# Matrix products over halves of the array's rows: inverse transforms, kernel rows and state sums of a long-convolution layer and its gradients, regrouped

## The chip, the cores and the metric

The kernel runs on one core of a Trainium2 chip. Its matrix engine (PE) multiplies, the vector engine (DVE) and the scalar engine (ACT) do elementwise work and empty the matrix engine's accumulators (PSUM), the general-purpose engine (POOL) and the sync engine (SP) mostly issue transfers. The metric is the device time of one execution in microseconds. The kernel before takes 607.57 us, the median of three runs (607.13 to 607.59).

## The reference, cut to what matters

The layer takes `u` of 2048 positions by 512 channels, normalises each position, and multiplies two branches: a state-space convolution, and a dense pair `w1` (512 by 1792) and `w2` with SiLU. The program returns the output and the gradients of eleven inputs.

```python
xn = layernorm(u)                                 # 2048 x 512
dt = exp(log_dt)[:, None]                         # 512 x 1
P  = exp((dt * A)[:, :, None] * arange(2048))     # 512 channels x 128 states x 2048 steps, complex
K  = einsum("dn,dnl,dn->dl", C, P, dt * B).real   # the convolution kernel, 512 x 2048
y  = irfft(rfft(pad(xn.T)) * rfft(pad(K)))[:, :2048].T + xn * Dskip
g  = silu(silu(xn @ w1) @ w2)
out = u + y * g
grads = vjp(out, grad_out)                        # of u, A, B, C, log_dt, Dskip, w1, w2
```

## The kernel before, in words

**Program order.** Every part of the work is a Python generator, called a stream, with a letter. A stream gives control back after each small piece: a group of matrix products, or the copy that empties a PSUM tile. `PLAN` holds seven strings, one for each section of the program, and `play` resumes the streams in the order of the letters. This is the order of each engine's instructions; nothing reorders them later. `SLOTS` says which buffer each new tile takes. `WAYS` says, stream by stream, which of the PSUM copies go to ACT (`A`) and which to DVE (`D`); all of them stand at one line of the profile for each engine (L112 for ACT, L113 for DVE).

**Forward section (to about 215 us).** The dense branch (`gen_ffn_fwd`: L751 and L768), the tables of powers, the kernel rows and the forward convolution run interleaved. The channels go in four bands of 128. A transform of length 4096 (`dft_fwd`) is a product over 128 positions (L405), sixteen transposes (L415), and a product with a small table `F2` (L425), which is 128 rows by 64 columns and is used twice, once for each half of the output's partitions. After it a spectrum tile has, on its 128 partitions, two halves of 64; each half holds 16 frequencies of 4 channels, so a 128-row slice of a spectrum holds 8 channels, 4 in each half.

**Inverse transforms** (`dft_inv`, 4 forward and 8 backward). The first step (L440) takes a spectrum slice of 128 by 128 as the stationary operand and a table `I2` of 128 by 256 as the moving one. `I2` carries the transform of 16 frequencies for 8 channels; a mask makes it zero wherever row and column belong to different channels, so it is zero between the two halves too. Four slices fill a PSUM tile of 1024 elements for each partition; one copy empties it into `dB`. The second step is L453.

**Kernel rows** (`gen_powers`, `gen_kernel_rows`). The 2048 powers of a channel come from 21 exponents `E` and 32 exponents `Y`. `Y[h]` (tile `YD`) is laid out as 16 groups of 4 channels: state on the partitions, then group, exponent, channel. For each group, L639 multiplies `Y` (128 states by 32 exponents of 4 channels) with `W` (21 exponents of 4 channels), four times, and accumulates. Of the 128 by 84 results those where the two channels are the same are wanted. Four groups fill a PSUM tile `ps_k` of 336 elements, and a copy moves it to `Xr`. The tables `SEL`, one for each of the 4 channels of a group, then pick and shift the wanted rows by further products (L651). The pool `pt` has one buffer, which `ps_k`, `ps_e` and later `psS` share in turn.

**Backward convolution (about 215 to 400 us).** Streams `D`, `B` and `E` transform the gradient, multiply spectra on DVE (`cplx_mul`, L466 to L474) and transform back, twice for each band. Between them run the backward products of the dense branch (L1149, L1169).

**State gradients (about 400 to 560 us).** `gen_ssm_fold` gathers the kernel's gradient (`GE`), sums it by products with `FO` (L953), and an ACT copy spreads it over 4 channels (`Gf`, L956). `gen_ssm_v` masks it with `MK` (`Gb`, L988, DVE), multiplies it with the transposed `Y` table (`YT`, L998, 168 columns for each of 256 products) and copies the result to `Vb`. DVE multiplies by `E` (`Tp`, L1013), and `gen_ssm_sums` adds the 21 exponents up by products with the identity into `psS` (L1031 to L1035: 43 products for each of 16 groups); ACT copies to `Sa` (L1037), and `gen_ssm_grads` works out the gradients. The two weight-gradient products (L1202, L1231) run beside this and on to the end, where the layer norm's gradient is finished (L1269 to L1293).

Of the kernel before, what the change touches and what calls it, by code (L numbers as in the profile page):

```python
# [31 lines left out]
XFXPPRRXRRFXXXJXQRRXFRRCCXXPRRPPJJPRCRCXRPFQRCCCQXXPCJCCQFFFQQFFFRFCCPPFFCCQFRQFFQQXFQCXQFFCFFFRRRCFFCCRRCJCCRRCCCRCRCPC
RCRXXFFQRCRXXXQQCRCXRCCXCXRQQRRRRXRQRXQQXQQFXRXPFXXXFFFCJCPFRFPPCCCCFFRRPPFXRQRRRFFFXUFQQQFFXCCFCCFQFCRRCUCQCCCFRQQRCCQR
QFCQFCCRRCCRRRRRCCRCCRRCRCCCCRRFFFFCRCCCCCRRRCRRCCRC/FCCCCFFCCCCCFGGFGGCCCCCGGGGGGFGFGCCCCGGGGGFFCFFFFFCFCCFFGWGGCCCCHHF
FGGGCCCCCFGCCFFCCCCCWCCCCHWGGWWWCCCHHHHHWWCWWWCCWCCWDMWWWDGDDWWDWWDDDWLWWWWDWDDDLCLLLMMMMDDDWWDD/dDDaDaddDDdDsAAAEADDDDD
BAaBAAaABBDEaAAsADDDAsABBBAABBBoooAoAAABBBsAAAEDBBADBlDBDAlAlBBBBBxBDABBBBOAooAxxDDoBDBABoAAOBBEBOBOOOOOlldlxaBxxBooBBBo
sxOooBBBBDDDDxoxoxBdDaxBBDBAABBBdBBBDDAAaBBBBOBBBBBBAABBsAAAOADDDEDAAADBAADOOoBsOdOBABOBAoAoAAABBBDoxAOAOODBABosBBABDxDB
BAoOBDDDDAADDAAODxDDooodDAOOOdoBBaOBBOBoBBoOOdodDDxDEDxxBxaBBBsAAAOOaAABBABABBDBDAABDBDBoBoBBxxDOOExDDDsxAABBxBABBaBABBs
AAABBABBEOOOxOxBAABBBABBABAxBBBxxaaaBBBBBAsBBBBBBBBBBBBAAAxxBBBAAABBBBBAAAABBBABdBd/xxdAdNssxxsYaAsAAAAYYNAAAAAAAxxNNAAA
AAAAAAYAAAAAANNxVVVVAAxVVVVVVAATTVVxxVVxVVYxVVTYYxxxxNNNTTTTNSVVVVVVVYxSx/VTTSTSVTTVVVVVhhVVVSSVVVVVVVTTTYYttTtSthVTTNTT  # L40
tttYwwtSVVVVSgVVVVtStthVtNNwNNwNVTwTTVVVwwNNNNZZTgStZSZZVtVVwVZtZtYYYhgvvYvvVZTTTTVVwVwZZVZVVSVVVVVYtTSTTTVvvwVttVVSVVVV
TTTvSTwgVVVhVVSYvtZZttwYYTTVThTVZtVVvZvZtVVVVVTSvvhVVVVSVVtSwwVVvVwTTTTwtTYYYVVVVZSSVTVVVZTTYtZZttZtvtVVVSVtTSVVVVvvVTgT
TZYZYTTwTVVVZZwvVVVZVZZVZhwwwSwStghtVVggVVSStwZgvVVZZVVhTTTvZZZTvTvTTSvvTvtSSStttvgthZvvwwttZZttZgZwwwZhZZZZvZvZZtttwwt/
wttivtiikkhvkwwikktkmkkmkkkmttmmmkimmvgkvvviigvvvvvwwkkmvttvkkkkwwvvkmkwkgmwwwkkimmkkmkmvmkmmmvvvvvvvvvmvkkkkmmmvmvvvvvv
vvvv
# [16 lines left out]

WAYS = """J=DAAAADDD;
F=AADAAAAAAAAADAAADAAAAAAAAAAADDAAAAAAADADAAAADAAADAAAAAAAADDAADADDDDDDDAA;
X=AAAADAAAAAAAAADAAAAAAAAAADAAAAAAAAAAAAAD;
R=AAAAAAADAADDADAAAAAAAAAAAAAAAADDDDDDDDAADAAADAAAAADDAAAAADAAAAAADAAAAAAADAAAADDA;
C=AADDAAAAAAAAAAAAAAAADDAAAAAAADAAADAAADAAAAADDADAADADDDADAAAAAAAA;
W=DDDDADDDDDDDDD;  # L70
D=AAAADDAAAADAAAAAAAAAAAAAADAAAADAADAAAAAA;
d=DDADAAAA;
# [1372 lines left out]
```

## Time and profile before

| | before |
|---|---|
| median of 3 runs | 607.57 us |
| the profiled execution | 606.76 us |
| its span, first to last instruction | 605.0 us |
| granted TensorE clock, mean over the span | 0.989 |
| instructions | 14383 |

The profiled execution lies 0.8 us below the median, and its span 1.8 us below its own time. In the profile a group of instructions is named by line, engine, operation and tiles; behind it stand how many there were, the time that they kept the engine busy and the mean time of one. A matrix product's printed duration has a modelled end and includes the way through the array: consecutive products overlap, and what one costs in a dense stretch is read from when the next one starts. In the timeline the first column is the start of a run of equal instructions, the second its length from the first start to the last modelled end; so the start of one row less the start of the row before it is what the earlier run cost. `PEld` is the loading of stationary operands.

### The profile page before, as it was taken

How to read it: one execution, taken by the hardware profiler on the slowest of the kernel's cores; microseconds unless marked ns; L12 is line 12 of the kernel's file. 1: busy time of each engine (PE TensorE's matmuls, PEld its weight loads, DVE VectorE, ACT ScalarE, POOL GpSimd, SP SyncE). 2: the span in 40 equal slices, each digit the busy share in tenths (PEclk: the TensorE clock that was granted, in tenths of full speed). 3: DMA queues.
4: the chain of work that ended last, by engine and by line, in shares of the span. 5: the costliest groups of instructions: out<-in, count | busy, mean ns of one | idle time of the engine just before them, and what ended most of it. 6: DMA issues, size and time to landing. Idle time of an engine off the chain costs nothing. (4 is left out here: it accounts for less than half of the span.)

```text
span 605.0 us, 14383 instructions
## 1 busy us (share of the span) xinstructions
PE 560.1 (93%) x5861; PEld 425.3 (70%) x5884; DVE 533.0 (88%) x906; ACT 443.2 (73%) x552; POOL 77.5 (13%) x171
## 2 busy tenths in 40 slices
PE   1597989999999989999999999999799999999995
PEld 1354758677777686786787767775787888795864
DVE  8989999999999889999998799568759889978894
ACT  7989989999998669998787864641575456434661
POOL 6211001010101120000000100000000202123121
PEclk9988999999999999999999999999999999999998
DMA  9896678676658598959877798797999999999993
GB/s 267 260 306 203 254 245 287 225 249 236 248 160 331 216 297 322 330 126 294 276 232 250 233 296 253 210 230 181 242 202 207 232 252 150 246 207 270 309 242 132
DMA packets 156066, 146.83 MB, mean 243 GB/s; under 512 B 79520, under 2 KB 133024, under 8 KB 152416
## 3 DMA queue, kind: packets, MB, share of 16 engines
q1 hardware_dynamic: 146688, 123.10, 72.1%
q0 software_dynamic: 6768, 19.93, 9.2%
q10 hardware_dynamic: 2544, 2.88, 1.5%
q8 instruction: 46, 0.75, 0.5%
q14 instruction: 20, 0.16, 0.1%
HBM read 63.44 MB, written 62.00 MB: 207 GB/s over the span
## 5 line engine op out<-in xcount | busy, mean ns | idle before, releaser
L112 ACT CAST dA<-ps_s 128x1024 bf16<-128x1024 f32 x86 | 86.3, 1037 | 7.6 <-PE ps_s L425 4.0
L751 PE MATMUL ps_h<-XT,W 128*128 128x256 bf16 x448 | 57.4, 279 | 6.2 <-ACT hT L112 4.6
L112 ACT CAST Vb<-ps_v 128x672 bf16<-128x672 f32 x49 | 34.1, 723 | 37.3 <-PE ps_v L998 32.7
L1149 PE MATMUL ps_da<-doT,W 128*128 128x256 bf16 x448 | 55.2, 273 | 1.2 <-ACT pd_s L112 1.1
L1013 DVE TENSOR_TENSOR Tp<-Vb,Eb 128x1344 bf16<-128x1344 bf16 x64 | 51.0, 850 | 5.9 <-ACT Vb L112 5.9
L768 PE MATMUL ps_o<-W,aT 128*128 128x512 bf16 x214 | 52.7, 399 | 1.1 <-issue 0.9
L112 ACT CAST dB<-ps_i 128x1024 bf16<-128x1024 f32 x41 | 41.1, 1031 | 16.4 <-PE ps_i L440 15.6
L751 PEld LDWEIGHTS <-W 128*128 128x128 bf16 x448 | 43.6, 100 | 12.9 <-issue 7.3
L1231 PE MATMUL ps_w<-dh_tok,xn 128*128 128x256 bf16 x448 | 51.8, 273 | 0.1
L1169 PE MATMUL ps_dx<-W,dhT 128*128 128x512 bf16 x224 | 50.8, 379 | 0.0
L1202 PE MATMUL ps_w<-YD,a_tok 128*128 128x512 bf16 x214 | 49.8, 379 | 0.5
L440 PE MATMUL ps_i<-I,sp_in 128*128 128x256 bf16 x384 | 47.3, 273 | 1.7 <-ACT dB L112 1.7
L1149 PEld LDWEIGHTS <-W 128*128 128x128 bf16 x448 | 42.8, 98 | 8.0 <-issue 2.8
L1231 PEld LDWEIGHTS <-xn 128*128 128x128 bf16 x448 | 43.2, 98 | 5.9 <-issue 0.5
L1152 DVE TENSOR_TENSOR dhT<-ps_da,dhT 128x512 bf16<-128x512 f32 x56 | 37.2, 684 | 10.3 <-PE ps_da L1149 7.3
L440 PEld LDWEIGHTS <-sp_in 128*128 128x128 bf16 x384 | 37.0, 98 | 8.9 <-DVE dB L113 1.9
L768 PEld LDWEIGHTS <-aT 128*128 128x128 bf16 x224 | 22.0, 102 | 29.3 <-issue 7.9
L1169 PEld LDWEIGHTS <-dhT 128*128 128x128 bf16 x224 | 21.3, 98 | 24.2 <-issue 1.2
L1202 PEld LDWEIGHTS <-a_tok 128*128 128x128 bf16 x224 | 21.5, 98 | 23.2
L466 DVE TENSOR_TENSOR cm<-sp_in,dA 128x2048 bf16<-128x2048 bf16 x24 | 29.3, 1219 | 4.9 <-DMA sp_in<-KXd 3.3
L425 PE MATMUL ps_s<-dB,F 128*64 128x512 bf16 x192 | 28.2, 388 | 3.8 <-ACT dB L112 2.1
L571 ACT ACTIVATE sn<-V 128x2048 bf16<-128x2048 int16 (+1 forms) x16 | 30.5, 1905 | 1.1 <-DVE V L567 1.1
(241 smaller groups left out, 1254.2 us busy)
## 6 DMA issues: line engine op xcount, KB each, us to landing
Yd<-YD SPq DMA_DIRECT2D x8, 1024.0 KB, 4.9
sp_in<-Ud SPq DMA_DIRECT2D x8, 1024.0 KB, 7.3
h_in<-Hd SPq DMA_DIRECT2D x14, 512.0 KB, 5.1
Ed<-E SPq DMA_DIRECT2D x8, 672.0 KB, 3.9
Eb<-Ed SPq DMA_DIRECT2D x8, 672.0 KB, 5.4
Hd<-hT POOLq DMA_DIRECT2D x8, 512.0 KB, 6.1
Ud<-dA SPq DMA_DIRECT2D x4, 1024.0 KB, 5.2
KXd<-dA SPq DMA_DIRECT2D x4, 1024.0 KB, 4.3
```

The lines of the kernel that those rows point to most:

```text
L112: return self.nc.scalar.copy(out=out, in_=in_)
L440: nc.tensor.matmul(out=ps[:, g], lhsT=Y[:, c, g0 + g, :], rhs=k.I2[:, c].rearrange("p c m -> p (c m)"), start=(c == 0), stop=(c == 1))
L466: TT(out=t2[:], in0=b[:, :, gs], in1=a[:, 1:2, gs].to_broadcast([P, 2, n, P]), op=ALU.mult)
L571: nc.scalar.activation(out=sn[:, 0:n], in_=low, func=ACT.Sin, scale=-2 * PI_LO / 2.0 ** PB)
L751: nc.tensor.matmul(out=ps[:, j], lhsT=k.W1[:, dk, ft * P:ft * P + P], rhs=XTv[:, :, dk, :], start=(dk == 0), stop=(dk == DK - 1))
L768: nc.tensor.matmul(out=ps[:], lhsT=aT[:, ft, t * P:t * P + P], rhs=k.W2[:, ft, :], start=(ft == 0), stop=(ft == FT - 1))
L1013: k.nc.vector.tensor_tensor(out=Tp[:, c, :, r ^ c].rearrange("p e (q w) a -> p q w e a", w=2), in0=Vb[:, :, c].rearrange("p q w (e a) -> p ...
L1149: nc.tensor.matmul(out=ps[:, j], lhsT=k.W2[:, ft, dk * P:dk * P + P], rhs=dTv[:, :, dk, :], start=(dk == 0), stop=(dk == DK - 1))
L1152: nc.vector.tensor_tensor(out=dh[:, i0:i0 + 2, :], in0=ps[:], in1=dh[:, i0:i0 + 2, :], op=ALU.mult)
L1169: nc.tensor.matmul(out=ps[:], lhsT=dhs[ft // 8][:, ft % 8, t * P:t * P + P], rhs=k.W1[:, :, ft * P:ft * P + P], start=(ft == 0), stop=(ft ...
L1202: nc.tensor.matmul(out=ps[:], lhsT=at[:, t, :], rhs=k.do[:, t, :], start=(t == 0), stop=(t == k.T - 1))
L1231: nc.tensor.matmul(out=ps[:], lhsT=k.xn[:, t, dk * P:dk * P + P], rhs=dh[:, t].rearrange("p j n -> p (j n)"), start=(t == 0), stop=(t == k ...
```

## The change

The tables and layouts are regrouped, so that products whose operands were half zero, or half unwanted, become pairs of smaller ones.

- `dft_inv`: the product with `I2` is done for each half of the 64 rows by itself: twice as many products, each with 64 rows and 128 columns in place of 128 rows and 256 columns. The two halves of a pair write to different PSUM banks. `I2` and its table work (`gen_step_tables`) have half the size.
- `Y` is laid out by 32 groups of 2 channels in place of 16 of 4. `gen_kernel_rows` multiplies each pair of channels by itself, into the upper or lower 64 output partitions: 1024 products of 64 output rows and 42 columns in place of 512 of 128 and 84. A PSUM tile now takes eight groups of 4, so there are half as many copies to `Xr`, of the same size. `SEL` has two tables for each kind in place of four, so there are 48 products at that place in place of 96. `E`, `W` and the products with them stay laid out by 4.
- `gen_powers`: the products that make `Y` and the helper `H` have rows of 2 elements where they had rows of 4.
- `gen_ssm_v`: as for the transforms, 64 rows and 84 columns, twice as many; `Gb`, `Gf` and `MK` have half the size; the copy to `Vb` writes it as before, laid out by 4.
- `gen_ssm_sums`: two exponents in one product, 23 products for each group in place of 43; `psS` and `Sa` have twice the size, and `gen_ssm_grads` adds their two halves.
- `PLAN`, `SLOTS` and `WAYS` are all replaced by new strings of the same kind (not shown).

```diff
 # setup_tiles, gen_plain_consts, gen_masks
-    k.SEL = k.p1.tile([P, 4, 4, 128], BF16, name="SEL")
+    k.SEL = k.p1.tile([P, 4, 2, 128], BF16, name="SEL")
+    G.memset(w.pairs[:], 0.0)
+    G.affine_select(out=w.pairs[:], in_=w.pairs[:], compare_op=ALU.not_equal, fill=1.0,
+                    base=0, pattern=[[2, 32], [64, 2], [1, 2]], channel_multiplier=-1)
-    for a in range(4):
+    for a in range(2):
         G.tensor_copy(out=lane(SEL[:, :, a])[:, :, :, a], in_=lane(MS[:])[:, :, :, a])
 # gen_step_tables
-    TT(out=sv[:], in0=sv[:], in1=mask[:].unsqueeze(1).to_broadcast([P, 3, 128]), op=ALU.mult)
+    TT(out=sv[:], in0=sv[:], in1=maskf[:].unsqueeze(1).to_broadcast([P, 3, 64]), op=ALU.mult)
 # dft_inv
-        ps = pc.tile([P, 4, 32, 8], F32, name="ps_i2", tag="pc")
+        ps = pc.tile([P, 2, 4, 32, 4], F32, name="ps_i2", tag="pc")
         for g in range(4):
             for c in range(2):
-                nc.tensor.matmul(out=ps[:, g], lhsT=Y[:, c, g0 + g, :], rhs=k.I2[:, c].rearrange("p c m -> p (c m)"),
-                                 start=(c == 0), stop=(c == 1))
+                for z in range(2):
+                    zs = slice(64 * z, 64 * z + 64)
+                    nc.tensor.matmul(out=ps[:, z, g], lhsT=Y[zs, c, g0 + g, :], rhs=k.I2[zs, c].rearrange("p c m -> p (c m)"),
+                                     start=(c == 0), stop=(c == 1))
         yield
-        ev(A2[:].rearrange("p c t (g e) -> p g (c t) e", e=8)[:, g0:g0 + 4], ps[:])
+        ev(A2[:].rearrange("p c t (g z e) -> p g z (c t) e", z=2, e=4)[:, g0:g0 + 4].rearrange("p g z x e -> p z g x e"), ps[:])
 # gen_powers
-    H = tbl.tile([P, 2, 16, 3, 4], BF16, name="H", tag="H")
+    H = tbl.tile([P, 2, 32, 3, 2], BF16, name="H", tag="H")
-    shp = [P, 16, 3, 8, 4]
+    shp = [P, 32, 3, 8, 2]
     lo = lambda c: Y[:, c, :, 0:8, :].unsqueeze(2).to_broadcast(shp)
     hi = lambda c: H[:, c].unsqueeze(3).to_broadcast(shp)
 # gen_kernel_rows
-            for u in range(2):
-                ps = k.pt.tile([P, 4, 84], F32, name="ps_k", tag="pt")
-                for q in range(4):
-                    for m in range(4):
-                        nc.tensor.matmul(out=ps[:, q], lhsT=Y[:, m % 2, q0 + 4 * u + q].rearrange("p j a -> p (j a)"),
-                                         rhs=W[:, m, 4 * u + q].rearrange("p e a -> p (e a)"), start=(m == 0), stop=(m == 3))
-                yield
-                qq = 16 * h + q0 + 4 * u
-                k.ev(Xr[:, :, :, qq:qq + 4], ps[:].rearrange("p q (e a) -> p a e q", a=4))
-                yield
+            ps = k.pt.tile([P, 8, NE * 2], F32, name="ps_k", tag="pt")
+            for q in range(8):
+                for m in range(4):
+                    for z in range(2):
+                        nc.tensor.matmul(out=ps[64 * z:64 * z + 64, q], lhsT=Y[:, m % 2, 2 * (q0 + q) + z].rearrange("p j a -> p (j a)"),
+                                         rhs=W[:, m, q, :, 2 * z:2 * z + 2], start=(m == 0), stop=(m == 3))
+                if q % 4 == 3:
+                    yield
+            qq = 16 * h + q0
+            k.ev(Xr[:, :, :, qq:qq + 8], ps[:].rearrange("p q (e a) -> p a e q", a=2))
+            yield
 # gen_ssm_fold
-                       in_=G21[:, bank, 0:32 * n].rearrange("p (e q) -> p q e", e=n).unsqueeze(3).to_broadcast([P, 32, n, 4]))
+                       in_=G21[:, bank, 0:32 * n].rearrange("p (e q) -> p q e", e=n).unsqueeze(3).to_broadcast([P, 32, n, 2]))
 # gen_ssm_v
-                    nc.tensor.matmul(out=ps[:, u, 168 * c:168 * c + 168], lhsT=YT[:, c, q + u, :],
-                                     rhs=Gb[:, q0 + q + u].rearrange("p w x -> p (w x)"), start=True, stop=True)
+                    for z in range(2):
+                        zs, x0 = slice(64 * z, 64 * z + 64), 168 * u + 84 * c
+                        nc.tensor.matmul(out=ps[:, z, x0:x0 + 84], lhsT=YT[zs, c, q + u, :],
+                                         rhs=Gb[zs, q0 + q + u].rearrange("p w x -> p (w x)"), start=True, stop=True)
-            k.ev(Vb[:, q:q + 2].rearrange("p q c w x -> p q (c w x)"), ps[:, :, 0:336])
+            k.ev(Vb[:, q:q + 2].rearrange("p u c w e (z a) -> p z u (c w e) a", z=2), ps[:, :, 0:336].rearrange("p z (u x a) -> p z u x a", u=2, a=2))
 # gen_ssm_sums
-        for e in range(NE):
-            nc.tensor.matmul(out=psS[:, 0:2], lhsT=k.ident[:], rhs=flat(Tp[:, 0, e]), start=(e == 0), stop=False)
+        for e in range(0, NE, 2):
+            n = min(2, NE - e)
+            add(n, 0, 2, Tp[:, 0, e:e + n], first=e == 0)
 ...
-        nc.scalar.copy(out=Sa[:, :, 16 * h + q0:16 * h + q0 + 8], in_=psS[:].rearrange("p r (q w a) -> p r q w a", w=2, a=4))
+        nc.scalar.copy(out=Sa[:, :, :, 16 * h + q0:16 * h + q0 + 8].rearrange("p z r q w a -> p (z r) q (w a)"),
+                       in_=psS[:].rearrange("p z r (q x) -> p (z r) q x", q=8))
 # gen_ssm_grads
+    TT(out=S[:, 0], in0=S[:, 0], in1=S[:, 1], op=ALU.add)
+    S = S[:, 0]
```

More of the change, by code (lines that the diff above doesn't have):

```diff
@@ L32 @@
[L32 to L36, printed above, removed]
@@ L80 @@
+V=AADDAAADDDDADADADAAAAAAADAAADDADAAAAAAAAAAAAAAAAAAADDAAAAAAAAAAA;
+w=AAAAAAAAAAADAA;
+v=ADAADADADDAADAAADDDAAAAAAADA"""
 class Placed:
@@ L170, in setup_tiles @@
     new("MS", [4, 128], BF16)
+    new("pairs", [128], BF16)
     new("il", [16], I32)
@@ L247, in gen_masks @@
     yield
[L248 removed]
+    I, J = k.ident, w.pairs
     par = lambda t: t.rearrange("p (r b a) -> p r b a", b=2, a=4)
[L250 to L253 removed]
+    pair = lambda t: t.rearrange("p (r b a) -> p r b a", b=2, a=2)
+    half = lambda t: t.rearrange("p (z x) -> p z x", z=2)
+    lane = lambda t: t.rearrange("p i (r a) -> p i r a", a=2)
+    G.tensor_copy(out=MS[:, 0], in_=J[:])
+    G.tensor_copy(out=MS[:, 1, 0:124], in_=J[:, 4:128])
+    G.tensor_copy(out=MS[:, 2, 124:128], in_=J[:, 0:4])
     yield
[L255 removed]
+    G.tensor_copy(out=par(MS[:, 3])[:, :, 0], in_=par(J[:])[:, :, 0])
     G.tensor_copy(out=par(MS[:, 3])[:, :, 1], in_=par(MS[:, 1])[:, :, 1])
     yield
[L258 removed]
+    for a in range(2):
         G.tensor_copy(out=lane(SEL[:, :, a])[:, :, :, a], in_=lane(MS[:])[:, :, :, a])
```

158 lines of the change are left out of this document (77 added, 81 removed).

## The prediction, written before the result was known

> **What bounds the kernel now.** First the page's busy shares, then the same by stage, cut where the sections change.
>
> ```profile
> span 605.0 us, 14383 instructions
> PE 560.1 (93%) x5861; PEld 425.3 (70%) x5884; DVE 533.0 (88%) x906; ACT 443.2 (73%) x552; POOL 77.5 (13%) x171
> ```
>
> ```profile
> core 0: us, PE busy (x) PEld busy (x) DVE busy (x) ACT busy (x) POOL busy (x), PEclk, DMA share, GB/s
> 0.00:100.00 100.00, 73.17 (x697) 51.15 (x702) 93.14 (x179) 92.29 (x122) 21.87 (x78) 0.95 0.80 252
> 100.00:215.00 115.00, 111.13 (x1285) 83.76 (x1291) 110.44 (x146) 104.21 (x136) 14.94 (x22) 1.00 0.68 243
> 215.00:400.00 185.00, 182.88 (x1842) 139.48 (x1842) 161.82 (x212) 143.41 (x143) 9.31 (x16) 1.00 0.83 261
> 400.00:450.00 50.00, 44.96 (x495) 34.60 (x494) 34.60 (x44) 22.51 (x31) 0.57 (x1) 1.00 0.89 211
> 450.00:560.00 110.00, 109.63 (x1242) 86.83 (x1247) 98.26 (x244) 58.76 (x87) 22.06 (x40) 1.00 1.01 223
> ```
>
> Up to 100 us DVE and ACT are full and PE idles for 27 us. From 100 to 215 PE, DVE and ACT are all nearly full, so that PE time alone buys little. From 215 to 400 PE is full and the others have slack. From 400 to 450 PE idles 5 us while the state gradients start. From 450 on PE is full and the transfers are at a share of 1.01, so they have no slack either. The waits confirm who is late:
>
> ```profile
> ACT Vb L112 <- PE ps_v L998: 32.7, 18, 6.4
> ACT dB L112 <- PE ps_i L440: 15.6, 12, 4.8
> PE ps_v L998 <- DVE Vb L113: 2.6, 2, 1.9
> ```
>
> In the inverse transforms the copy waits for PE (15.6 us in 12 waits); for `Vb` too, but there PE also waits for copies between 400 and 450.
>
> **What a product costs.** From the timeline of PE, start of one run to the start of the next:
>
> ```profile
> 119.57 1.04 PE L440 MATMUL ps_i<-I,sp_in 128*128 128x256 bf16 x8
> 120.45 0.77 PE L639 MATMUL ps_k<-W,YD 128*128 128x84 bf16 x16
> 121.05 1.03 PE L751 MATMUL ps_h<-XT,W 128*128 128x256 bf16 x8
> 121.92 0.61 PE L405 MATMUL ps_s<-xn,TF 128*128 128x128 bf16 x8
> 122.37 1.03 PE L651 MATMUL ps_e<-Xr,SEL 128*128 128x512 bf16 x3
> ...
> 408.64 1.03 PE L1169 MATMUL ps_dx<-W,dhT 128*128 128x512 bf16 x4
> 409.50 0.74 PE L998 MATMUL ps_v<-Gb,YT 128*128 128x168 bf16 x8
> 410.08 1.04 PE L1149 MATMUL ps_da<-doT,W 128*128 128x256 bf16 x8
> ```
>
> Eight products of 256 columns take 0.88, eight of 128 0.45, sixteen of 84 0.60, eight of 168 0.58, four of 512 0.86: 0.110, 0.056, 0.0375, 0.0725 and 0.215 us each, about 0.42 ns a column and 2.5 ns more. Loads of operands are hidden even at 84 columns.
>
> What half of the array does is seen at L425, whose table is 64 columns wide:
>
> ```profile
> 135.06 0.62 PE L425 MATMUL ps_s<-dB,F 128*64 128x512 bf16 x4
> 135.61 0.62 PE L134 MATMUL pt_t<-ident,xn 128*128 128x128 bf16 x8
> 136.16 0.62 PE L425 MATMUL ps_s<-dB,F 128*64 128x512 bf16 x4
> ...
> 50.27 0.14 PEld L425 LDWEIGHTS <-F 128*64 128x64 bf16 x4 [0.21 <-issue]
> ...
> L425 PEld LDWEIGHTS <-F 128*64 128x64 bf16 x192 | 8.2, 108 | 14.0 <-issue 10.4
> ...
> 425.27 0.22 PE L1033 MATMUL psS<-Tp,ident 128*128 128x64 bf16 x2
> 425.32 1.28 PE L1035 MATMUL psS<-Tp,ident 128*128 128x128 bf16 x20
> ```
>
> Four products of 512 columns take 0.55, where four in turn would take 0.86 and two 0.43: the two column halves run together. The 0.12 above 0.43 is the way into this form, and the eight transposes behind it take 0.55 where 0.45 is usual, so the way out costs 0.10: **0.11 us for each switch**. Four loads lie within 0.14 us, each printed at 0.108, so they begin within 0.03 us: about 0.027 for the two rounds. The smallest full products seen, 64 columns, take 0.05 for two, 0.025 each.
>
> **The change part by part: PE.**
>
> - *Inverse transforms.* 48 groups of 8 products, 0.88 each. After: 8 pairs of 128 columns. If row halves run together as column halves do, 8 x 0.056 = 0.45; in turn, 0.90. No product on row halves is in this trace; its nearest row is L425, so I take 0.45. 16 groups forward: -6.9; 32 backward: -13.8.
> - *Kernel rows.* 32 groups of 16 products, 0.60. After: 16 pairs of 42 columns. Bounds: 0.020 (columns alone) and 0.05 (two smallest products in turn); between them lie the loads of L425, 0.027, and this is the same form, so I take it. 32 x (0.60 - 0.43) = -5.4; by the bounds -9 to +6.4.
> - *`SEL`.* Half the products of these groups:
>
> ```profile
> L651 PE MATMUL ps_e<-Xr,SEL 128*128 128x512 bf16 x13 | 4.0, 379 | 0.5 <-DVE Xr L113 0.3
> L651 PE MATMUL ps_e<-Xr,SEL 128*128 128x224 bf16 x32 | 3.7, 259 | 0.0
> L651 PE MATMUL ps_e<-Xr,SEL 128*128 128x128 bf16 x32 | 2.4, 219 | 0.0
> L651 PE MATMUL ps_e<-Xr,SEL 128*128 128x160 bf16 x16 | 1.8, 232 | 0.9 <-DVE KE L113 0.9
> ```
>
>   With 16 at 512 (three are not recorded), at 0.42 ns a column and 2.5 each: 9.4, so -4.7.
> - *`ps_v`.* 64 groups of 4 products, 0.29. After: 4 pairs of 84 columns, 0.15 (0.20 at 0.05 a pair, 0.30 in turn): -9.0; by the bounds -5.8 to +0.6.
> - *Sums.* 41 of 128 columns and 2 of 64, 2.35, become 19 of 256 and 4 of 128, 2.31: 16 groups, about -0.7.
> - *Switches.* Counted in the order of the changed program: 84, 79 and 55 in the forward, backward and last sections, against 46, 28 and 0. 38, 51 and 55 more at 0.11: +4.2, +5.6, +6.1.
>
> PE in all: forward -12.8, backward -8.2, last part -3.6.
>
> [...]
>
> **DVE, ACT, POOL, transfers.**
>
> ```profile
> L112 ACT CAST Xr<-ps_k 128x336 bf16<-128x336 f32 x28 | 13.2, 471 | 1.2 <-PE ps_k L639 1.2
> L113 DVE CAST Xr<-ps_k 128x336 bf16<-128x336 f32 x4 | 2.0, 499 | 0.8 <-PE ps_k L639 0.8
> L988 DVE TENSOR_TENSOR Gb<-Gf,MK 128x2688 bf16<-128x2688 bf16 x8 | 12.4, 1546 | 0.0
> L956 ACT CAST Gf<-G 128x2048 bf16<-128x2048 f32 x4 | 7.5, 1867 | 6.3 <-PE G L953 6.3
> L1072 DVE TENSOR_TENSOR Sa<-Sa 128x256 f32<-128x256 f32 x4 | 1.7, 415 | 2.3 <-ACT Sa L1037 2.3
> L1037 ACT COPY Sa<-psS 128x192 f32<-128x192 f32 x16 | 5.2, 326 | 16.0 <-PE psS L1035 16.0
> L609 DVE TENSOR_TENSOR m<-YD,H 128x1536 bf16<-128x1536 bf16 x16 | 15.2, 950 | 0.2
> ```
>
> `Xr`: 32 copies become 16 (15 on ACT, 1 on DVE): ACT -13 x 0.471 = -6.1, DVE -3 x 0.499 = -1.5. Smaller step tables save DVE an estimated 1 us at the start. `Gb` halves: -6.2 on DVE. The new sum of `Sa` halves is three times the 0.415 row at most: 4 x 1.25 = +5.0. `Gf` halves: ACT -3.8. `Sa` copies twice as large: at most 16 x 0.33 = +5.2 on ACT, hidden, since ACT is busy 59 of 110 us there; without that cover each would delay the next `psS`. Copies to `Vb` and `dB` keep their size and cost 0; their shorter runs are hidden in the element rate, at worst some ns each. Products with rows of 2 (L609 and its like) I cost at 0; see the third rival. POOL's extra mask build lies in its idle time (22 of 100 us busy). Transfers keep their sizes and number, apart from where the order puts them.
>
> **The sum.** Forward: DVE and ACT lose 8.6 us together, so 4.3 each when shared; they were as full as PE, so 4.3 of PE's 12.8 shows: **-4.3**. Backward: PE is the bound, -8.2, but the chain transform, product on DVE, transform does not shorten on DVE: two thirds, **-5.5** (0 to -8.2). Last part: -3.6 on PE and about -2 on the starting chain (`Gf` -0.9, `Gb` -0.8), but the transfers are full: **-2** (0 to -5). Together -11.8 against the profiled 606.76, that is 595; 0.8 more against the median of 607.57: **596 us**, own range 588 to 603.
>
> **The rivals.**
>
> 1. *Small products are bound by loads or issue* (0.05 a pair): kernel rows +6.4, so forward PE is -6.9 + 6.4 - 4.7 + 4.2 = -1.0 and shows no gain worth more; `ps_v` -5.8 leaves the last part at -0.4. Only about -1 and the backward -5.5 stay: 601. For it: 0.025 is the smallest product seen. Against: L425's 0.03 for four loads.
> 2. *Row halves run in turn*, the slower side. Inverse groups 0.90, `ps_v` 0.30, switches still paid: backward +0.6 + 5.6 = +6.2, last part +0.6 - 0.7 + 6.1 = +6.0, forward -4.3: 607.6 + 7.9 = 615. It decides from a pair of 128 columns at about 0.08 us upwards. For it: no row shows such a pair. Against: column halves overlap, and the pairs write to different banks. [...]
> 3. *Rows of 2 halve DVE's rate.* L609 does 1536 elements in 0.950, more than one a ns, with rows of 4. At half the rate the 32 products of its kind cost some 0.8 more each, +26, on a DVE that is full there: about 630. For it: no such row is in the trace. Against: the elements still come in adjacent pairs. [...]
> 4. *The gain is hidden anyway*: the new order ends elsewhere, transfers or DVE hold the last part, 606 to 609.
>
> **How the numbers follow.** Forecast 0.58; rival 1 0.17; rival 2 0.11; rival 3 0.05; rival 4 0.09. 0.2% (1.2 us) is about what a measurement can tell from no change. Faster: the forecast, nearly all of rival 1: 0.73. Same: 0.06, most of rival 4. Slower: rivals 2, 3 and the rest of 4, 0.21. The range takes in rivals 1 and 4 and half of 2: 586 to 612.
>
> **What would show it.** Right: groups of 16 half products at L444 take 0.45 to 0.55 us; 32 at L643 about 0.45; PE busy from 215 to 400 ends some 8 us earlier; `m<-YD,H` stays at 0.95. Wrong: L444 near 0.9, L643 above 0.8, or PE waiting for DVE or transfers behind 215 us where it did not.

## The result, and the profile after

The changed kernel takes 603.28 us (median of 7 runs, 600.19 to 605.27), the kernel before in the same comparison 607.59 us (606.13 to 609.22). The ratio is 0.9924, with a 95% interval of 0.9896 to 0.9951: it is faster, by 0.8%, some 4.3 us. The forecast was 11.6 us. The profiled execution took 603.28 us and its span is 601.5 us, 3.5 us below the span before.

The page of the changed kernel, its first lines:

```profile
span 601.5 us, 15937 instructions
PE 542.6 (90%) x6645; PEld 392.8 (65%) x6668; DVE 524.2 (87%) x894; ACT 438.8 (73%) x550; POOL 75.5 (13%) x169
```

PE is busy 17.5 us less than before, DVE 8.8 us and ACT 4.4 us. The span is only 3.5 us shorter. So work is gone, for PE less than the 24.6 us to which its terms in the prediction add up, and most of the time is not. By stage, with the columns of the prediction's table:

```profile
0.00:100.00 100.00, 70.28 (x759) 48.03 (x765) 89.18 (x169) 87.98 (x116) 19.88 (x76) 0.93 0.80 244
100.00:215.00 115.00, 108.20 (x1756) 78.67 (x1758) 110.37 (x141) 104.44 (x132) 11.45 (x15) 0.99 0.72 246
215.00:400.00 185.00, 178.14 (x2197) 131.34 (x2199) 163.93 (x219) 144.43 (x149) 12.89 (x23) 1.00 0.85 269
400.00:450.00 50.00, 45.81 (x518) 30.75 (x518) 34.96 (x58) 25.29 (x36) 0.57 (x1) 1.00 1.00 217
450.00:560.00 110.00, 107.70 (x1172) 78.45 (x1172) 95.09 (x238) 61.48 (x94) 23.08 (x42) 1.00 1.06 230
```

In the first 100 us every engine does less than before: PE 70 us in place of 73, DVE 89 in place of 93, ACT 88 in place of 92. An engine that does less in a stage where it was the limit is waiting for something. That is where the gain went. The windows are cut at fixed times, however, while the sections move, so four milestones are better: the last `ds` (end of the forward section), the last `ps_dx` (end of the backward section), the last `psS` (end of the state sums) and the last `ps_w`. In each row the end is the start plus the length. The timeline of the kernel before:

```profile
239.85 3.08 DVE L804 TENSOR_TENSOR ds<-Gr,g 128x1024 bf16<-128x1024 bf16 x5
416.53 6.21 PE L1169 MATMUL ps_dx<-W,dhT 128*128 128x512 bf16 x28
541.26 1.28 PE L1035 MATMUL psS<-Tp,ident 128*128 128x128 bf16 x20
584.03 14.54 PE L1231 MATMUL ps_w<-dh_tok,xn 128*128 128x256 bf16 x128
```

and of the changed kernel:

```profile
244.04 3.09 DVE L809 TENSOR_TENSOR ds<-Gr,g 128x1024 bf16<-128x1024 bf16 x5
415.93 3.18 PE L1185 MATMUL ps_dx<-W,dhT 128*128 128x512 bf16 x14
533.13 2.46 PE L1040 MATMUL psS<-Tp,ident 128*128 128x256 bf16 x23
593.19 1.91 PE L1247 MATMUL ps_w<-dh_tok,xn 128*128 128x256 bf16 x16 [0.34 <-ACT o L111]
```

| stretch (us) | before | after | difference | forecast |
|---|---|---|---|---|
| start to the last `ds` (forward) | 242.9 | 247.1 | **+4.2** | -4.3 |
| to the last `ps_dx` (backward) | 179.8 | 172.0 | **-7.8** | -5.5 |
| to the last `psS` (state sums) | 119.8 | 116.5 | -3.3 | -2 for both |
| to the last `ps_w` (tail) | 56.0 | 59.5 | +3.5 | |
| to the end of the span | 6.4 | 6.4 | 0 | |

The backward section did better than forecast. The forward section became longer where it should have become shorter, and the last part gave back in its tail what it had won.

Four things stand in the forward section. The first is the start. This is the chain of waits of the changed kernel, its first 28 us:

```profile
1.31 0.17 POOL pairs L219
...
1.56 0.87 POOL pairs L220
2.43 0.15 POOL zero L222
2.72 0.09 POOL il L228
2.81 0.20 POOL jf L229
3.03 1.23 DVE prod L281
...
6.19 1.28 ACT L322
...
9.54 12.06 ACT mag_all L512 x23
```

POOL's new mask `pairs` stands ahead of the index table `jf`; the new order has DVE begin with `prod`, which needs `jf`; behind that come the step tables, the sines of ACT and then the magnitudes. They run from 9.5 to 27.7 us, where they ran from 8.5 to 25.7.

The second is SP's queue, here in its timeline after:

```profile
35.91 3.30 SPq L518 DMA_DIRECT2D Md<-mag_all  x3
39.31 10.02 SPq L291 DMA_TRANSPOSE TI<-TF  x1
49.38 0.58 SPq L588 DMA_DIRECT2D mag<-Md  x1
```

and before:

```profile
33.47 3.48 SPq L514 DMA_DIRECT2D Md<-mag_all  x3
37.05 8.93 SPq L287 DMA_TRANSPOSE TI<-TF  x1
46.02 0.59 SPq L584 DMA_DIRECT2D mag<-Md  x1
```

The load of `mag`, from which DVE makes the first `E`, is issued behind the transposing transfer into `TI`, which holds the queue for 10 us. It is issued 3.4 us later than before. DVE was ready for it at nearly the same time in both kernels, at 49.9 and 49.6 us, as its timeline shows, before and after:

```profile
50.59 1.63 DVE L598 TENSOR_TENSOR E<-sn,mag 128x2048 bf16<-128x2048 bf16 x2 [0.67 <-DMA mag<-Md]
```

```profile
53.74 1.63 DVE L602 TENSOR_TENSOR E<-sn,mag 128x2048 bf16<-128x2048 bf16 x2 [4.15 <-DMA mag<-Md]
```

A wait of 0.67 us has become one of 4.15, on the engine that is fullest in this section.

The third is the rate of DVE. Its groups before, by shape:

```profile
L598 DVE TENSOR_TENSOR YD<-sn,mag 128x896 bf16<-128x896 bf16 x8 | 4.9, 616 | 0.0
L598 DVE TENSOR_TENSOR H<-sn,mag 128x384 bf16<-128x384 bf16 x8 | 2.8, 349 | 0.0
```

and after:

```profile
L602 DVE TENSOR_TENSOR YD<-sn,mag 128x896 bf16<-128x896 bf16 x8 | 7.6, 947 | 0.0
L602 DVE TENSOR_TENSOR H<-sn,mag 128x384 bf16<-128x384 bf16 x8 | 3.6, 452 | 0.0
L613 DVE TENSOR_TENSOR m<-YD,H 128x1536 bf16<-128x1536 bf16 x16 | 15.3, 953 | 0.2
L993 DVE TENSOR_TENSOR Gb<-Gf,MK 128x1344 bf16<-128x1344 bf16 x8 | 6.8, 850 | 1.0 <-ACT Gf L961 1.0
L1086 DVE TENSOR_TENSOR Sa<-Sa 128x768 f32<-128x768 f32 x4 | 3.8, 954 | 3.1 <-ACT Sa L1050 3.1
```

The products that write `Y` and `H` in scattered rows of 2 take 0.33 and 0.10 us more each, 3.5 us in all. `m<-YD,H`, whose inputs are rows of 2 that lie next to each other or are read again, keeps its 0.95.

The fourth is the granted clock of PE, the third number from the end of a windows row. From 50 to 100 us it is 0.97 before and 0.90 after, from 150 to 215 us 1.00 and 0.97, and in the changed kernel it is 0.66 from 180 to 185 us. What such a stretch can cost is seen in two kernels of the next section that have the same code up to the end of the forward section (`TI` and `pairs` later, and fewer loads). Their rows from 170 to 180 us:

```profile
170.00:180.00 10.00, 7.29 (x114) 4.60 (x114) 8.96 (x11) 9.95 (x11) 0.57 (x1) 1.00 0.70 223
170.00:180.00 10.00, 7.29 (x47) 3.43 (x46) 6.72 (x10) 7.49 (x8) 0.56 (x1) 0.66 0.67 215
```

The same copy of `ps_h` starts on DVE at 177.22 us in the first and at 179.36 in the second, behind a wait of 3.24 us for PE, and the two forward sections end at 240.0 and 241.7 us. So 1.7 us between two profiles of this section can be no more than the clock, and a part of the +4.2 may be. Why the clock falls there is not shown.

### The profile page after: what moved, and what is told of

The parts are those of the page before. It is cut to its first block, busy times and chain, and to the rows that moved or that the text cites. A ratio compares the mean times of both kernels' runs of the same rounds, so it can differ in the third digit from the quotient of the medians.

```text
span 601.5 us, 15937 instructions
## 1 busy us (share of the span) xinstructions
PE 542.6 (90%) x6645; PEld 392.8 (65%) x6668; DVE 524.2 (87%) x894; ACT 438.8 (73%) x550; POOL 75.5 (13%) x169
## 4 chain that ended last, share of the span: by engine, by line
PE 36%; DVE 33%; ACT 11%; DMA 10%; issue 6%; SPq 2%; POOL 1%; DVEq 0%; POOLq 0%; ACTq 0%
PE ps_dx L1185 5%; PE ps_da L1165 5%; PE psS L1040 5%; PE ps_w L1218 4%; DVE cm L470 4%; PE ps_w L1247 3%; DVE sp_in L472 3%; PE ps_h L756 3%; ACT mag_all L512 3%; DMA YD<-Od 2%; DVE dhT L1168 2%; ACT sn L575 2%; PE pt_t L133 2%; PE ps_v L1005 2%; PE ps_s L427 2%
## 5 line engine op out<-in xcount | busy, mean ns | idle before, releaser
L111 ACT CAST dA<-ps_s 128x1024 bf16<-128x1024 f32 x83 | 83.1, 1042 | 5.6 <-PE ps_s L427 3.2
L756 PE MATMUL ps_h<-XT,W 128*128 128x256 bf16 x448 | 61.3, 291 | 4.7 <-ACT hT L111 2.2
L1165 PE MATMUL ps_da<-doT,W 128*128 128x256 bf16 x448 | 56.1, 273 | 0.0
L756 PEld LDWEIGHTS <-W 128*128 128x128 bf16 x448 | 44.6, 104 | 16.1 <-issue 7.9
L1247 PE MATMUL ps_w<-dh_tok,xn 128*128 128x256 bf16 x448 | 51.7, 273 | 2.5 <-ACT o L111 2.0
L773 PE MATMUL ps_o<-W,aT 128*128 128x512 bf16 x215 | 50.3, 384 | 1.2 <-issue 0.9
L111 ACT CAST dB<-ps_i 128x1024 bf16<-128x1024 f32 x42 | 42.1, 1027 | 12.2 <-PE ps_i L444 12.1
L1247 PEld LDWEIGHTS <-xn 128*128 128x128 bf16 x448 | 43.0, 98 | 8.6 <-issue 3.2
L1040 PE MATMUL psS<-Tp,ident 128*128 128x256 bf16 (+1 forms) x368 | 39.5, 264 | 1.2 <-ACT Sa L1050 1.2
L111 ACT CAST o<-ps_w 128x256 bf16<-128x256 f32 (+1 forms) x31 | 13.9, 463 | 32.6 <-PE ps_w L1218 19.6
L1040 PEld LDWEIGHTS <-ident 128*128 128x128 bf16 x368 | 33.1, 98 | 5.4 <-issue 1.2
L427 PE MATMUL ps_s<-dB,F 128*64 128x512 bf16 x192 | 30.0, 401 | 6.7 <-ACT dB L111 3.3
```

What stands on the lines that cost most here:

```text
L111: return self.nc.scalar.copy(out=out, in_=in_)
L427: nc.tensor.matmul(out=ps[64 * h:64 * h + 64, 4 * v:4 * v + 4], lhsT=k.F2[:, c, :], rhs=Bv[:, u, h, 4 * v:4 * v + 4, :], start=True, stop= ...
L756: nc.tensor.matmul(out=ps[:, j], lhsT=k.W1[:, dk, ft * P:ft * P + P], rhs=XTv[:, :, dk, :], start=(dk == 0), stop=(dk == DK - 1))
L773: nc.tensor.matmul(out=ps[:], lhsT=aT[:, ft, t * P:t * P + P], rhs=k.W2[:, ft, :], start=(ft == 0), stop=(ft == FT - 1))
L1040: nc.tensor.matmul(out=out, lhsT=k.ident[:], rhs=rhs.rearrange("p z r x a -> p z (r x a)"), start=first, stop=last)
L1165: nc.tensor.matmul(out=ps[:, j], lhsT=k.W2[:, ft, dk * P:dk * P + P], rhs=dTv[:, :, dk, :], start=(dk == 0), stop=(dk == DK - 1))
```

## The experiments

The explanation under test: the PE part of the forecast holds, and the forward section lost its gain to the new order (the transfer into `TI`, the mask) and to the rows of 2. Theories A and B are those that each run's own expectation states. All were compared with the kernel before on their own chip, where it took 607.6 to 609.2 us; so the ratios and the stretches of the profile are to be compared, rather than the microseconds of two lines of this table.

| kernel | median us | ratio, 95% interval | to `ds` | `ds` to `ps_dx` | to `psS` | to `ps_w` |
|---|---|---|---|---|---|---|
| changed kernel | 603.28 | 0.9924 [0.9896, 0.9951] | 247.1 | 172.0 | 116.5 | 59.5 |
| `TI` later | 597.69 | 0.9823 [0.9793, 0.9853] | 241.2 | 171.9 | 115.6 | 61.8 |
| rows of 4, cleared | 602.23 | 0.9890 [0.9860, 0.9919] | 246.5 | 172.0 | 117.4 | 59.5 |
| before, with inverse halves | 606.96 | 0.9972 [0.9952, 0.9993] | 243.4 | 177.0 | 119.8 | 56.0 |
| inverse products full | 611.39 | 1.0052 [1.0030, 1.0075] | 250.2 | 178.4 | 114.7 | 59.6 |
| `TI` and `pairs` later | 595.29 | 0.9780 [0.9758, 0.9802] | 240.0 | 172.0 | 114.6 | 61.6 |
| output order | 602.98 | 0.9898 [0.9867, 0.9930] | 244.7 | 172.0 | 115.8 | 61.8 |
| before, with `TI` later | 606.65 | 0.9962 [0.9947, 0.9976] | 241.3 | 179.7 | 121.4 | 56.1 |
| `ps_v` full | 602.66 | 0.9913 [0.9880, 0.9947] | 247.6 | 172.2 | 115.9 | 59.0 |
| `Y` by four | 594.88 | 0.9764 [0.9733, 0.9794] | 237.9 | 172.0 | 117.8 | 57.5 |
| fewer loads | 593.91 | 0.9752 [0.9726, 0.9778] | 241.7 | 172.0 | 114.6 | 57.5 |
| `Cr`, `Ci` first | 592.92 | 0.9751 [0.9729, 0.9773] | 238.6 | 172.0 | 115.2 | 58.9 |

### The transfer into `TI`, later

```diff
 # gen_tables (its last step stays, empty)
-    nc.sync.dma_start_transpose(k.TI[:], k.TF[:].rearrange("p t c k -> p (t c k)"))
 # gen_first_powers, after the memsets: behind the first load of mag
+    k.nc.sync.dma_start_transpose(k.TI[:], k.TF[:].rearrange("p t c k -> p (t c k)"))
```

> The changed kernel with one transfer moved: the transpose that makes TI (issued by SP ahead of the first load of mag, 10 us of the queue) is issued behind that load. Theory A (the forward section is set by the chain magnitudes, Md, mag, DVE products, and in the changed kernel DVE stands still for 4.15 us for that load): the wait goes, the section ends 3 to 4 us earlier, 599 to 600 us. Theory B (PE sets the forward section too, and its gain was eaten by switches of form and a colder clock at the start): no change, 603.

597.69 us, and the forward section ends at 241.2 us in place of 247.1. The first `E` of this kernel, in its timeline, starts without a wait:

```profile
49.63 1.19 DVE L602 TENSOR_TENSOR E<-sn,mag 128x2048 bf16<-128x2048 bf16 x1
```

4.1 us came out of one wait, and 5.9 us out of the section, more than the wait itself and more than the 3 to 4 of theory A. Of the rest, 0.9 us are there on DVE by 126 us. Behind that the clock is low at different times (0.66 from 180 to 185 us in the changed kernel, from 210 to 215 us here), so what is left is not ascribed. By the ratios one transfer's place in a queue was worth 1.0%, more than the whole measured gain of the change.

### Rows of 4 in the products that write `Y` and `H`

```diff
 # gen_first_powers
+    k.nc.vector.memset(k.Y[0], 0.0)
+    k.nc.gpsimd.memset(k.Y[1], 0.0)
 # gen_powers: the same memory, viewed by four
-            parts = (..., (Y[:, :, :, 1:8, :], 5, 12, 2), (H[:], 12, 15, 2))
+            parts = (..., (Y4[:, :, :, 1:8, :], 5, 12, 4), (H4, 12, 15, 4))
```

The powers that are formed are not the wanted ones, so this run tells of time alone.

> The changed kernel with the products that make Y and H (YD<-sn,mag and H<-sn,mag) writing rows of 4 again, as in the kernel before, into the same memory; the powers then lie at other places than the readers expect, so the kernel computes other values, and YD is cleared once at the start. Theory A: DVE gets back 8 x (0.31 + 0.07) = 3 us in a section that DVE sets, 600 to 601 us. Theory B: no change, 603.

602.23 us. `Y` and `H` are back at 618 and 379 ns, but the clearing made DVE wait 2.6 us for POOL, so the run tells the rate and not its worth. It was tried again below without the clearing.

### The kernel before, with the inverse transforms by halves alone

```diff
 # dft_inv, I2 and its tables as in the change; PLAN, SLOTS and WAYS of the kernel before
```

> The kernel before with one part of the change alone: inverse transforms by halves and their smaller tables, the order of before untouched. PE's time for it falls by 48 groups x (0.87 - 0.55) less the way in, 0.096 for those not side by side: 3 to 4 us forward, 7 to 8 backward. Theory A: only the backward part shows, 600 to 602 us. Theory B: both parts show, 596 to 597 us.

606.96 us, 0.3% faster: both theories missed, which had 600 to 602 and 596 to 597. The backward section is 2.8 us shorter, in place of the 7 to 8 expected, and the rest is as it was within 0.5 us. In the old order PE then waits in small pieces in that section: for `doT`, `dhT` and `sp_in`, 0.9 to 1.4 us each, which are not among its waits in the kernel before.

### The changed kernel, with the inverse products over the full array

```diff
 # dft_inv: one product with 128 rows and 256 columns, the table's columns read twice
-                for z in range(2):
-                    zs = slice(64 * z, 64 * z + 64)
-                    nc.tensor.matmul(out=ps[:, z, g], lhsT=Y[zs, c, g0 + g, :], rhs=k.I2[zs, c]..., ...)
+                nc.tensor.matmul(out=..., lhsT=Y[:, c, g0 + g, :], rhs=k.I2[:, c]....to_broadcast([P, 2, 128]), ...)
```

The two halves of the table are added together here, so the inverse transforms are not the reference's.

> The changed kernel with the inverse transforms' products at the full 128 rows and 256 columns again (the table is read twice, so the values are not the transform's), the order of the changed kernel untouched. Theory A: the backward section gives its gain back, 7 to 8 us, the forward one stays, 609 to 611 us. Theory B: 11 us, 613 to 615 us.

611.39 us, 8 us more than the changed kernel: 3.1 in the forward section and 6.4 in the backward one (178.4 against 172.0), with 1.8 less up to `psS`. So the forward section did not stay, as theory A had it, and the 11 us of theory B are too many. The stretch from `ds` to `ps_dx` is 171.9 to 172.2 us in every kernel with the new order and the halves, whatever was done ahead of it. So in the new order the halves account for 6.4 of the 7.8 us there, and the rest of the change for 1.4.

### `TI` later, and the mask later

```diff
 # gen_plain_consts: the two instructions of pairs, behind the last index table
+    G.memset(w.pairs[:], 0.0)
+    G.affine_select(out=w.pairs[:], in_=w.pairs[:], compare_op=ALU.not_equal, fill=1.0, ...)
     yield
```

> The earlier experiment (transpose into TI later) with POOL's build of `pairs` moved behind the index tables. Theory A, that the first 10 us are a chain and the build of 1.05 us stands on it: the magnitudes begin at 8.5 and end at 26.7 in place of 27.7, the forward section ends 0.7 to 1 us earlier, 596.7 to 597.0. Theory B, that what DVE and ACT have queued behind it takes up the delay: the magnitudes begin earlier, but the forward section and the time stay within 0.3 us of 597.7.

595.29 us. The forward section ends 1.2 us earlier, a little more than theory A has it, and the magnitudes run from 8.1 to 26.2 us. The instructions of DVE are 1.1 to 1.4 us ahead from 8 us up to the end of the section, with the same clock in both kernels (1.00 from 50 to 100 us, 0.97 from 150 to 215), so this is the mask's. The median fell by twice that, but the intervals of the two ratios overlap. The stretches behind `ds` differ between the two kernels by less than the same code differs elsewhere in the table (the tail 57.5 to 61.8), so the rest isn't ascribed.

### Output order

```diff
 # gen_powers, in the kernel with TI later
-            TT(out=eq(o), in0=qe(sn[:, i0:i1], na), in1=qe(m, na), op=ALU.mult)
+            for c in range(2):      # Y and H only
+                TT(out=o[:, c], in0=qo(sn[:, i0:i1, c], na), in1=qo(mag[:, x0 + i0:x0 + i1], na), op=ALU.mult)
```

> The same earlier experiment with the products that write Y and H cut in two by real and imaginary part and walked in the order of the output, so that writes run on in 14 and 6 elements and the reads are rows of 2. Theory A, that the scattered writes of 4 bytes cost the 0.33 us: two halves take 0.62 to 0.75 together (0.31 to 0.37 each, with one more fixed part), the DVE has 1.5 to 2.5 us less to do in the forward section and the time falls by 1 to 2 us, to 596. Theory B, that any row of 2 on the side of sn and mag costs it, read or written: the halves take 0.47 each or more, and the time stays at 597.7 or goes up by up to 1 us.

602.98 us, theory B and worse: the halves of `Y` take 0.613 us each, against 0.95 for the whole, and those of `H` 0.267 against 0.45. Now both inputs are read in scattered rows of 2, and for `Y` this costs more than the scattered writes did. DVE is kept busy 1.6 us longer by them (9.2 + 3.6 against 7.6 + 3.6), and the forward section is 3.5 us longer. The clock is lower too (0.97 against 1.00 from 50 to 100 us, 0.95 against 0.97 from 150 to 215), so what the other 1.9 us are stays open.

### The kernel before, with `TI` later

```diff
 # the edit of the first experiment, in the kernel before
```

> The kernel before, with its transpose into TI moved behind the first load of mag, as in the earlier experiment. Theory A, that the changed kernel lost its forward gain to its own order of the queue: the kernel before has only 0.7 us of waiting for that load, so it gains 0.3 to 1 us, 607 to 608.5 against 608.9. Theory B, that moving the transpose is a good thing in any order and has nothing to do with the change: it gains as much as the changed kernel did, 5 to 6 us, 603.

606.65 us: 0.4% faster (2.6 us by the medians), between the two theories. Its forward section is 1.6 us shorter, all of it from the first `E` on, against 5.9 in the changed kernel. So the transfer's place costs the kernel before something as well, and about 4 us of its price are the change's own order.

### `ps_v` over the full array

```diff
 # gen_ssm_v
-                    for z in range(2):
-                        zs, x0 = slice(64 * z, 64 * z + 64), 168 * u + 84 * c
-                        nc.tensor.matmul(out=ps[:, z, x0:x0 + 84], lhsT=YT[zs, c, q + u, :], rhs=Gb[zs, q0 + q + u]..., ...)
+                    nc.tensor.matmul(out=ps[:, u, 168 * c:168 * c + 168], lhsT=YT[:, c, q + u, :],
+                                     rhs=Gb[:, q0 + q + u]....to_broadcast([P, 2, 84]), start=True, stop=True)
```

> The changed kernel with the products into ps_v over all 128 rows and 168 columns again (the other half's columns read twice, so its state gradients are wrong and only the time counts). By the row of the kernel before a group of four takes 0.29 where the changed one takes 0.15 and its way in and out. Theory A, that PE bounds the last part: 64 groups cost 4 to 6 us less the 28 ways in and out of 0.19, so 0 to +3 us net, and the end of ps_v moves as much as the end of the kernel. Theory B, that the ways in and out eat the whole gain: within 0.6 us of the changed kernel, with the order of the waits as it is. Theory C, that transfers bound the last part: ps_v ends later, the kernel's end stays within 0.5 us.

602.66 us, the same as the changed kernel within the intervals, and the stretch to `psS` is 115.9 us against 116.5. PE is busy 547.1 us in place of 542.6, and 1.7 us of that lie between 450 and 560 us. In the kernel before four full products take 0.29 us and eight 0.58, where the pairs take 0.26 and 0.41 with their way out; that shows nowhere in the end. The smaller groups pay their way in as well (0.10 us: sixteen products of L1247 take 1.85 ahead of a pair and 1.75 ahead of full products), and what is left may be taken up by waits. This is theory B. For theory C `ps_v` would have to end later; its last product ends 101.9 us behind the last `ps_dx`, against 102.3 in the changed kernel.

### `Y` and `H` by four

```diff
 # gen_powers, in the kernel with TI and pairs later; k.Y is viewed as "p c q j a" with q=16, a=4
-    H = tbl.tile([P, 2, 32, 3, 2], BF16, name="H", tag="H")
+    H = tbl.tile([P, 2, 16, 3, 4], BF16, name="H", tag="H")
-            parts = (..., (Y[:, :, :, 1:8, :], 5, 12, 2), (H[:], 12, 15, 2))
+            parts = (..., (Y[:, :, :, 1:8, :], 5, 12, 4), (H[:], 12, 15, 4))
 # gen_kernel_rows
-  lhsT=Y[:, m % 2, 2 * (q0 + q) + z].rearrange("p j a -> p (j a)")
+  lhsT=Y[:, m % 2, q0 + q].rearrange("p j a -> p (j a)")[:, 64 * z:64 * z + 64]
```

> The last version (transpose into TI later, `pairs` later) with Y and H laid out by 4 channels as in the kernel before, so that all products that write or read them have rows of 4; the kernel rows' products take 64 columns of Y that lie together, so the powers that they use are not the wanted ones, and only the time counts. Nothing has to be cleared for it. Theory A, that writing rows of 2 costs 0.33 and 0.10 us a product and that DVE holds the forward section: YD back at 0.62 and H at 0.35, the DVE 3.5 us less, the forward section 2.5 to 4 us shorter, 591.5 to 593. Theory B, that the waits behind it take the gain up: YD and H as in A, but the time within 1 us of 595.3.

Its groups of DVE, by shape:

```profile
L602 DVE TENSOR_TENSOR YD<-sn,mag 128x896 bf16<-128x896 bf16 x8 | 4.9, 617 | 0.0
L602 DVE TENSOR_TENSOR H<-sn,mag 128x384 bf16<-128x384 bf16 x8 | 3.0, 378 | 0.0
```

The rate is back, and DVE has 3.3 us less to do. The forward section ends at 237.9 us, 2.1 us earlier. Of that 1.7 us are there by 166 us (the `sp_in` that starts at 166.36 us in the kernel before this edit starts at 164.70 here); from 150 to 215 us the clock is 1.00 here and 0.97 there, so the last 0.4 may be the clock's. In the time of the whole kernel this can't be told from nothing: 594.88 us over a wide spread (590.43 to 601.89), a ratio of 0.9764 against 0.9780, with intervals that overlap. So the cost of the rows of 2 is shown on DVE and in the forward section of a profile, and not in the time.

### Half of the weight gradients' loads left out

```diff
 # gen_dw2_loads, gen_dw1_loads, in the kernel with TI and pairs later
+        if ft % 2:
+            k.h[ft] = k.h_last      # likewise k.dht[f] = k.dh_last
+            yield
+            continue
```

> The same version with every second load of h_in and of dh_tok left out and the tile before used again, so the weight gradients are wrong and only the time counts. It takes 3.5 MB of 7 and half of the transposing transfers of dh_tok out of the last section, whose share of transfer time is 1.06. Theory A, that transfers hold the last section (from the end of the backward products to the end, 176 us in all kernels so far): it becomes 4 to 8 us shorter, 588 to 591. Theory B, that PE with its ways in and out holds it up to the end of the state sums and the copies and layer-norm steps hold the rest: within 1 us of 595.3.

Window of the kernel with `TI` and `pairs` later, and then of this one:

```profile
450.00:560.00 110.00, 108.30 (x1173) 81.06 (x1177) 96.19 (x233) 61.66 (x94) 24.48 (x44) 1.00 1.04 231
```

```profile
450.00:560.00 110.00, 108.25 (x1175) 80.62 (x1180) 96.11 (x233) 62.38 (x95) 24.09 (x44) 1.00 0.80 185
```

The transfers' share falls from 1.04 to 0.80 and nothing else moves; the stretch to `psS` is 114.6 us in both. Transfers at a share of 1.0 do not hold the last part up to there. The tail is 57.5 us in place of 61.6, but it is 57.5 in `Y` by four too, with all its loads; so whether the loads had a part in the tail stays open. The time, 593.91 us, lies between the two theories, and the forward section, whose code is untouched, is the one that ended 1.7 us later at a lower clock.

### `Cr` and `Ci` ahead of the magnitudes' stores

```diff
 # PLAN, section 0: the last "p" (loads of Cr and Ci on SP) moved directly behind the third
-...767766p666F57666FFFFFF777FFp465777644
+...767766pp666F57666FFFFFF777FF465777644
```

> The same version with the loads of Cr and Ci put ahead of the first three stores of the magnitudes on SP. Theory A, that the chain to the first phases goes through Ci (it lands 5 us after the magnitudes end, and the products into CT stand ahead of the phases on DVE): the first product into E begins 2 to 4 us earlier and the time falls by 1.5 to 3 us, to 592.3 to 593.8. Theory B, that the stores of the magnitudes then wait behind the transposing loads: no gain, or up to 1 us slower.

592.92 us lies where theory A has it, but the intervals of 0.9751 and 0.9780 overlap, so the time does not show a gain. The first product into `E` begins 1.0 us earlier (47.4 in place of 48.4, less than the 2 to 4 expected), and DVE keeps that lead up to 212 us. The forward section ends 1.4 us earlier, at 238.6 us, with the clock at 1.00 from 150 to 215 us in place of 0.97. This is the fastest version here that leaves nothing out, 2.5% below the kernel before. Its three edits move instructions and leave every product as it is; together they are worth 1.7%, twice the change's own 0.8%. The first of them is worth 0.4% in the kernel before as well.

## Why the prediction was wrong, step by step

The forecast was 596 us and the time is 603.28; the sign was right and the wide range (586 to 612) held, the own range (588 to 603) just missed, and the size was not right.

*PE, inverse transforms.* Right. In the timeline of PE after, a run costs the start of the next row less its own start:

```profile
125.78 0.62 PE L444 MATMUL ps_i<-I,sp_in 64*128 64x128 bf16 x16 [0.26 <-ACT dA L111]
126.33 1.92 PE L756 MATMUL ps_h<-XT,W 128*128 128x256 bf16 x16
128.19 0.82 PE L444 MATMUL ps_i<-I,sp_in 64*128 64x128 bf16 x16
128.94 0.69 PE L643 MATMUL ps_k<-W,YD 128*64 128x42 bf16 x32
129.55 1.05 PE L756 MATMUL ps_h<-XT,W 128*128 128x256 bf16 x8
```

Eight pairs take 0.55 us with the way out (forecast 0.45 without it), against 0.88 for the eight full products before. In turn it would have been 0.90: row halves run together, and rival 2 falls. What the different banks do for this was not shown, since no run has the two row halves of a pair in one bank.

*PE, kernel rows.* Near in the price, and it gained nothing. The 32 products at L643 take 0.61 us with the way out. Where two groups stand together, 64 take 1.03:

```profile
147.63 1.19 PE L643 MATMUL ps_k<-W,YD 128*64 128x42 bf16 x64
148.66 0.60 PE L427 MATMUL ps_s<-dB,F 128*64 128x512 bf16 x4
```

L427 behind them has column halves too, so this 1.03 has no way out in it: 0.032 a pair, where 0.027 was forecast from a row of loads that itself has 0.14 less 0.108, or 0.032. Sixteen pairs are then 0.51 of the 0.61, and the way out 0.10. The way in shows in the row ahead, as at L756 above: 1.86 for 16 products that take twice 0.88 elsewhere, 0.10 more. So a group with both ways takes longer than the 0.60 of the sixteen full products before. The forecast had both terms, -5.4 here, which becomes -2.8 at 0.032, and +4.2 for the switches of the forward section; its -4.3 for that section came from DVE and ACT and does not change by this. Rival 1, with 0.05 a pair, falls.

*PE, `ps_v` and sums.* Right in the price; for `ps_v` the run over the full array shows no gain, and the sums were not tried alone. Four pairs with the way out take 0.26 us and 23 sums 2.40, in the timeline:

```profile
440.39 0.33 PE L1005 MATMUL ps_v<-Gb,YT 64*128 64x84 bf16 x8
440.65 2.47 PE L1040 MATMUL psS<-Tp,ident 128*128 128x256 bf16 x23
443.05 0.48 PE L1005 MATMUL ps_v<-Gb,YT 64*128 64x84 bf16 x16
```

*"Forward ... -4.3".* This is the step that failed: measured +4.2. The step priced the work of each engine and not its place in the order. "POOL's extra mask build lies in its idle time" was wrong: POOL is idle later, but at 1.3 us it stands on the chain to the magnitudes, and moving it gave 1.2 us. That the transfer into `TI` is in the queue ahead of the first load of `mag` was given no price, only the words "apart from where the order puts them": moving it gave 5.9 us. The rows of 2, "I cost at 0", are 3.5 us of DVE and 1.7 to 2.1 us of the section. With the three undone the section ends at 237.9 us, 5.0 us earlier than in the kernel before and 3.4 earlier than in the kernel before with `TI` later; the forecast of 4.3 for the work itself lies between. The clock is a term that the prediction did not have. Its share of the +4.2 stays open, and of the three parts the mask's alone was seen at the same clock throughout.

*Rival 3* was right that rows of 2 cost DVE time, and wrong in place and size. It let them cost 26 us in the products that read them. Those kept 0.95; the products that write them paid, 3.5 us: 0.33 us more for 896 elements (947 less 616 ns) and 0.10 more for 384 (452 less 349). Why the scattered rows cost that is not shown.

*"Backward ... -5.5".* Measured -7.8, near the end of its range that takes the whole PE saving. Of it 6.4 are the halves and 1.4 the rest of the change. "Two thirds" for the chain between transform and product was too cautious in the new order; in the old one, where the halves gave 2.8, it was too much. The waits behind it, here of ACT for PE, shrank from 15.6 us:

```profile
ACT dB L111 <- PE ps_i L444: 12.1, 13, 2.4
```

*"Last part ... -2".* Measured 0.2. To the end of the state sums it gained 3.3. That this is close to the 3.6 of PE's sum is luck at least in part, since that sum counts on `ps_v`, and with `ps_v` over the full array the stretch is no longer. The tail gave 3.5 back: PE waits for `o` there (2.0 us for ACT and 0.5 for DVE), where before no such wait stood. Up to the state sums "the transfers are full" was no reason, as the run with fewer loads shows. The new sum at L1086 costs 0.95 each, 3.8 us, where at most 5.0 was forecast; the halved `Gb` gave 5.6 us, where 6.2 was. The copies to `dB` and `Vb`, costed at 0, take 1027 and 733 ns each on ACT, where they took 1031 and 723. What sets the tail between 57.5 and 61.8 us in kernels with the same code there isn't settled.

*Rivals 1 and 4* come nearest in the number, with 601 and 606, and both by luck: a pair does not take the 0.05 us of rival 1, and nothing hid the gain as in rival 4; another cost was paid beside it. The numbers of the outcome are -7.8 + 0.2 + 4.2 = -3.4 against -11.8.

## What to carry to other kernels

When a change brings a new order of the program, price the first 60 us by hand, queue by queue: moving a build of 1 us from ahead of an index table and one transposing transfer from ahead of a load gave 7 us in the forward section here, not much less than the 9.5 us that the halved products of the inverse transforms gained in the two sections. Compare the granted clock of two profiles before a difference of 2 us is given to an edit. "The engine is 22% busy" says nothing of an instruction's place; ask what stands behind it on its queue and who waits for that. Splitting products that are half zero pays where groups are long enough to carry their way in and out (some 0.2 us together here): it did for eight pairs of 128 columns, and by their rows it did not for sixteen of 42 or four of 84.

## What the runs showed of the hardware that was not expected

A DVE product of 896 elements of 2 bytes took 616 ns with output rows of 4 and 947 ns with scattered output rows of 2; one of 384 took 349 and 452. With rows of 2 scattered on both inputs and output that runs on in 14 elements, 448 elements took 613 ns. With rows of 2 on inputs that lie next to each other or are read again, nothing changed (0.95 us for 1536).

Products on row halves that write to different PSUM banks begin in pairs every 0.056 us at 128 columns (eight pairs take 0.55 us and sixteen 0.99, with the way out), and pairs on column halves every 0.032 us at 42 columns (32 take 1.03), less than the 0.0375 us of one full product of 84 columns.

The granted clock fell for short stretches in the midst of a busy section, at other times in other kernels: 0.66 over 170 to 180 us in one, 1.00 over the same 10 us of the same code in another.
